# Opening each head's turn with its own block transposes in a streaming attention-backward kernel

## Chip, cores and metric

One core of one Trainium2 chip. The metric is the device time of one execution in microseconds (us). Every number below is of runs in the state called fast; no profiled run fell into another state.

## The reference

Attention with one query per head, and its gradients: 32 heads, 8,192 keys, head size 128, bf16.

```python
def _fwd_reference(q, k, v):                       # q: 1,32,1,128   k, v: 1,32,8192,128
    scale = q.shape[-1] ** -0.5
    scores = jnp.einsum('bhqd,bhkd->bhqk', q, k) * scale
    attn = _softmax(scores, axis=-1)
    return jnp.einsum('bhqk,bhkd->bhqd', attn, v)

def reference(q, k, v, grad_out):                  # cut
    _out, _vjp = jax.vjp(_fwd_reference, q, k, v)
    return (_out, *_vjp(grad_out))                 # out, dq, dk, dv
```

K and V are read once, dK and dV written once: four tensors of 67 MB (64 MiB), 8.39 MB for each head. There is little arithmetic on them.

## The kernel before

One head takes one turn of the loop. Its work is: block transposes of K on the vector engine (`k_blocks`), scores on PE, softmax, V transposed on PE (`v_transposes`), products of V with the output gradient (`v_scores`), then dv as an outer product. dk and dq of a head need a sum over all its products, so they run in the next head's turn. All transfers are issued from one queue: K into three buffers, V into two, each gradient stored in two pieces of 1 MB.

```python
K_BUFS, V_BUFS, NST = 3, 2, 2

for h in range(H + 1):                 # before; softmax details cut
    p_ = h - 1
    k_scores(h); v_transposes(h, 1)
    ds_of(p_); outer(p_, "dk", 0)
    s_mask(h); s_swap(h)
    outer(p_, "dk", 1)                 # stores the first half of dk
    k_blocks(h + 1, 0)                 # next head's K, one stage ahead
    v_transposes(h, 2)
    # ... maximum and its broadcast ...
    v_scores(h, 1)
    outer(p_, "dk", 2); outer(p_, "dk", 3)
    dq_of(p_)                          # last use of K of the head before
    load_k(h + 2)
    # ... exponentials ...
    k_blocks(h + 1, 1); k_blocks(h + 1, 2)
    # ... sum, probabilities, v_transposes(h, 3), v_scores(h, 2) ...
    contract(Vt.pop(h), x["p"], x["m"][:, 2:3])
    for r in range(4):
        outer(h, "dv", r)
    v_scores(h, 3)
    load_v(h + 2)
    v_transposes(h + 1, 0); k_blocks(h + 1, 3); v_scores(h + 1, 0)
```

## Time and profile before

| | before |
|---|---|
| time, median of 3 runs | 675.39 us (674.85 to 675.66) |
| span of the profiled run | 672.6 us |
| one turn, heads 8 to 30 | 20.5 us |

A turn is measured here from the start of one head's masking instruction (the one that writes `sm`) to the next head's.

```profile
180.00:340.00 160.00, 129.75 (x2642) 119.45 (x2640) 123.25 (x156) 41.26 (x79) 0.00 (x0) 0.50 1.01 409
345.00:625.00 280.00, 222.44 (x4584) 205.15 (x4582) 215.41 (x274) 72.75 (x138) 0.00 (x0) 0.54 1.01 411
```

A transfer's completion is recorded once per DMA engine, 16 times in all. Below, **lag** is how much later the last engine finishes a load than the first. The completion records are in the trace, but in none of the page's tables.

### The profile page before, as it was taken

How to read it: one execution, taken by the hardware profiler on the slowest of the kernel's cores; microseconds unless marked ns; L12 is line 12 of the kernel's file. 1: busy time of each engine (PE TensorE's matmuls, PEld its weight loads, DVE VectorE, ACT ScalarE, POOL GpSimd, SP SyncE). 2: the span in 40 equal slices, each digit the busy share in tenths (PEclk: the TensorE clock that was granted, in tenths of full speed). 3: DMA queues.
4: the chain of work that ended last, by engine and by line, in shares of the span. 5: the costliest groups of instructions: out<-in, count | busy, mean ns of one | idle time of the engine just before them, and what ended most of it. 6: DMA issues, size and time to landing. Idle time of an engine off the chain costs nothing.

```text
span 672.6 us, 23041 instructions
## 1 busy us (share of the span) xinstructions
PE 524.4 (78%) x10727; PEld 483.7 (72%) x10727; DVE 508.7 (76%) x658; ACT 172.4 (26%) x321; POOL 0.7 (0%) x6
## 2 busy tenths in 40 slices
PE   3788897878888787878787887878787888877783
PEld 3687786767777777777777777767777777777682
DVE  4678896777787877877777778768777678687766
ACT  1323322222222223222222222222222222222320
POOL 0000000000000000000000000000000000000000
PEclk9975656565555555555555555656556565566665
DMA  8899999999999999999999999999999999999976
GB/s 338 370 382 422 419 427 418 422 427 424 405 410 414 409 411 393 421 416 402 406 412 405 413 413 409 402 416 409 423 419 399 423 399 415 413 396 417 391 292 252
DMA packets 29808, 269.96 MB, mean 401 GB/s; under 512 B 3472, under 2 KB 3472, under 8 KB 6032
## 3 DMA queue, kind: packets, MB, share of 16 engines
q1 hardware_dynamic: 29712, 268.48, 97.6%
q8 instruction: 84, 1.38, 0.8%
q14 instruction: 12, 0.10, 0.0%
HBM read 134.23 MB, written 134.23 MB: 399 GB/s over the span
## 4 chain that ended last, share of the span: by engine, by line
DMA 64%; PE 23%; DVE 8%; ACT 3%; issue 1%; SPq 1%; ACTq 0%; DVEq 0%
DMA Kt<-in_k_dram 64%; PE dp_ps L185 8%; PE T_ps L168 5%; DVE XK_sb L133 5%; PE m_ps L256 3%; PE dp_ps L180 3%; ACT XT_sb L170 2%; PE m_ps L185 1%; PE s_ps L145 1%; DVE diag L254 1%; DVE G_dv L195 1%; DVE G_dk L195 1%; PE m_ps L276 0%; DVE mx L252 0%; ACT p_rep L282 0%
## 5 line engine op out<-in xcount | busy, mean ns | idle before, releaser
L168 PE MATMUL T_ps<-ident,Vt 128*128 128x128 bf16 x2048 | 238.3, 310 | 1.1 <-DMA Vt<-in_v_dram 1.1
L168 PEld LDWEIGHTS <-Vt 128*128 128x128 bf16 x2048 | 218.5, 150 | 7.0 <-issue 5.4
L170 ACT COPY XT_sb<-T_ps 128x1024 f32<-128x1024 f32 x128 | 129.5, 1012 | 334.2 <-PE T_ps L168 334.2
L195 DVE TENSOR_TENSOR G_dv<-p_rep,qd 128x2048 bf16<-128x2048 bf16 x128 | 148.2, 1221 | 77.5 <-ACT p_rep L282 63.4
L133 DVE STREAM_TRANSPOSE XK_sb<-Kt 128x1024 f32<-128x1024 f32 x128 | 155.1, 1230 | 57.2 <-DMA Kt<-in_k_dram 57.2
L195 DVE TENSOR_TENSOR G_dk<-ds_rep,qd 128x2048 bf16<-128x2048 bf16 x128 | 153.2, 1219 | 1.1
L180 PEld LDWEIGHTS <-XT_sb 128*128 128x128 bf16 x2048 | 72.5, 106 | 45.1 <-ACT XT_sb L170 43.8
L180 PE MATMUL dp_ps<-doT,XT_sb 128*128 128x1 bf16 x2048 | 75.1, 166 | 35.3 <-ACT XT_sb L170 35.3
L185 PE MATMUL m_ps<-p_rep,Vt 128*128 128x1 bf16 x2048 | 59.0, 165 | 37.0 <-ACT p_rep L282 37.0
L185 PEld LDWEIGHTS <-Vt 128*128 128x128 bf16 x2048 | 59.5, 104 | 39.0 <-issue 39.0
L145 PE MATMUL s_ps<-q_blk,XK_sb 128*128 128x4 bf16 x2048 | 59.1, 168 | 0.0
L185 PE MATMUL dp_ps<-ds_rep,Kt 128*128 128x1 bf16 x2048 | 58.2, 164 | 0.7 <-issue 0.5
L145 PEld LDWEIGHTS <-XK_sb 128*128 128x128 bf16 x2048 | 57.1, 104 | 0.0
L185 PEld LDWEIGHTS <-Kt 128*128 128x128 bf16 x2048 | 56.2, 101 | 0.8 <-issue 0.6
L256 PE MATMUL m_ps<-diag,ones_f 128*128 128x128 f32 x64 | 21.5, 431 | 38.1 <-DVE diag L254 38.1
L256 PEld LDWEIGHTS m_ps<-diag,ones_f 128*128 128x128 f32 x64 | 13.9, 270 | 45.1 <-DVE diag L254 45.1
L276 PEld LDWEIGHTS m_ps<-rs,ones_f 128*128 128x128 f32 x64 | 15.9, 309 | 25.2 <-ACT qd L211 25.2
L276 PE MATMUL m_ps<-rs,ones_f 128*128 128x1 f32 x64 | 18.6, 360 | 16.4 <-ACT qd L211 16.4
L224 ACT COPY dq_all<-dp_ps 128x1 f32<-128x1 f32 x32 | 5.1, 159 | 93.4 <-PE dp_ps L185 93.4
L151 DVE TENSOR_TENSOR sm<-s_ps,in_quad 128x256 f32<-128x256 f32 x32 | 13.6, 425 | 12.3 <-PE s_ps L145 12.3
L287 ACT COPY o_all<-m_ps 128x1 f32<-128x1 f32 x32 | 5.1, 159 | 61.8 <-PE m_ps L185 61.8
L291 PE MATMUL m_ps<-o_all,do_f 128*128 128x1 f32 x64 | 18.1, 352 | 0.0
(40 smaller groups left out, 160.2 us busy)
## 6 DMA issues: line engine op xcount, KB each, us to landing
Kt<-in_k_dram SPq DMA_DIRECT2D x31, 2048.0 KB, 15.9
out_dram<-G_dv SPq DMA_DIRECT2D x62, 1024.0 KB, 11.8
out_dram<-G_dk SPq DMA_DIRECT2D x62, 1024.0 KB, 11.9
Vt<-in_v_dram SPq DMA_DIRECT2D x30, 2048.0 KB, 16.4
Vt<-in_v_dram SPq DMA_DIRECT2D x8, 512.0 KB, 11.2
Kt<-in_k_dram SPq DMA_DIRECT2D x4, 512.0 KB, 5.2
out_dram<-G_dv SPq DMA_DIRECT2D x4, 512.0 KB, 3.4
out_dram<-G_dk SPq DMA_DIRECT2D x4, 512.0 KB, 4.6
```

Source lines behind the costliest of these rows:

```text
L133: nc.vector.transpose(XK[h][:, :, :, u, :], slots(Kt[h], u, NCH).rearrange("p g d -> p (g d)").bitcast(F32).rearrange("p (g w j) -> p g w ...
L145: nc.tensor.matmul(out[:, g, :], lhsT=cols[:, g, c // 2, c % 2], rhs=q_blk[:, h, c, :], start=(c == 0), stop=(c == 2 * NB - 1), skip_group ...
L151: nc.vector.tensor_tensor(x["sm"][:], x["s"][:, 0:NT].rearrange("p (a g) -> p a g", a=NQ).unsqueeze(2) .to_broadcast([P, NQ, NCH, CH]), in ...
L168: nc.tensor.transpose(T_ps[:, i, :], Vt[h][:, c * CH + i, :], ident[:])
L170: nc.scalar.copy(X.rearrange("p c s -> p (c s)").bitcast(F32), T_ps.rearrange("p c s -> p (c s)").bitcast(F32))
L180: nc.tensor.matmul(st[h]["dp"][:, n:n + 1], lhsT=X[:, i, :], rhs=doT[:, h:h + 1], start=True, stop=True, skip_group_check=True)
L185: nc.tensor.matmul(out_col, lhsT=Xt[:, n, :], rhs=rep[:, n, 0:1], start=(n == 0), stop=(n == NT - 1), skip_group_check=True)
L195: nc.vector.tensor_tensor(slots(G, r, 4).rearrange("p n (a b) -> p n a b", b=R), slots(rep, r, 4).unsqueeze(2).to_broadcast([P, Q, D // R, ...
L254: nc.vector.tensor_scalar(diag[:], ident_f[:], mx[:], scale, op0=ALU.mult, op1=ALU.mult)
L256: nc.tensor.matmul(x["m"][:, 128:256], lhsT=ones_f[:], rhs=diag[:], start=True, stop=True, skip_group_check=True)
L276: nc.tensor.matmul(x["m"][:, 0:1], lhsT=ones_f[:], rhs=rs[:], start=True, stop=True, skip_group_check=True)
L291: nc.tensor.matmul(x["m"][:, 1:2], lhsT=do_f[:, h:h + 1].to_broadcast([P, P]), rhs=o_all[:, h:h + 1], start=True, stop=True, skip_group_ch ...
```

## The change

The intent: one pipeline stage less. A head's block transposes open its own turn, so K is needed later and the first head starts sooner; dq follows its `ds` at once, in two halves; K and V are requested as their buffers fall free, V ahead of the second half of the dv store. The core of it (cut):

```diff
+    def dq_of(h, half):
+        out = st[h]["dp"][:, 128:129]
+        contract(Kt[h], st[h]["ds"], out, half * NT // 2, (half + 1) * NT // 2)
 ...
-            k_scores(h)
+            x = st[h] = {}
+            for u in range(NCH):
+                k_blocks(h, u)
+            v_transposes(h, 0)
             v_transposes(h, 1)
+            k_scores(h)
+            v_scores(h, 0)
 ...                                   (ds, dk 0, mask, swap)
+            dq_of(p_, 0)
             outer(p_, "dk", 1)
-            if more:
-                st[h + 1] = {}
-                k_blocks(h + 1, 0)
-            v_transposes(h, 2)
 ...                                   (maximum)
+            dq_of(p_, 1)
+        if 0 < h and h + 2 < H:
+            load_k(h + 2)
             outer(p_, "dk", 2)
 ...                                   (exponentials, sum)
             outer(p_, "dk", 3)
-            dq_of(p_)
-        if h + 2 < H:
-            load_k(h + 2)
-            k_blocks(h + 1, 1)
-            k_blocks(h + 1, 2)
 ...                                   (V: transposes 2, contraction, products, transposes 3)
-        for r in range(4):
-            outer(h, "dv", r)
         v_scores(h, 3)
+        outer(h, "dv", 0)
+        outer(h, "dv", 1)
         if h + 2 < H:
             load_v(h + 2)
-        if more:
-            v_transposes(h + 1, 0)
-            k_blocks(h + 1, 3)
-            v_scores(h + 1, 0)
+        outer(h, "dv", 2)
+        outer(h, "dv", 3)
```

More of the change, by code (lines that the diff above doesn't have):

```diff
@@ L181, in v_scores, with contract @@
                              start=True, stop=True, skip_group_check=True)
-    def contract(Xt, rep, out_col):
-        for n in range(NT):
+    def contract(Xt, rep, out_col, first=0, last=NT):
+        for n in range(first, last):
             nc.tensor.matmul(out_col, lhsT=Xt[:, n, :], rhs=rep[:, n, 0:1],
@@ L220, in ds_of @@
             in1=x["p_s"][:].unsqueeze(2).to_broadcast([P, NT, R]), op0=ALU.subtract, op1=ALU.mult)
-    def dq_of(h):
-        contract(Kt.pop(h), st[h]["ds"], st[h]["dp"][:, 128:129])
-        nc.scalar.copy(dq_all[:, h:h + 1], st[h]["dp"][:, 128:129])
-    st[0] = {}
-    for u in range(NCH):
-        k_blocks(0, u)
-    v_transposes(0, 0)
-    v_scores(0, 0)
+    def dq_of(h, half):
+        out = st[h]["dp"][:, 128:129]
+        contract(Kt[h], st[h]["ds"], out, half * NT // 2, (half + 1) * NT // 2)
+        if half == 1:
+            nc.scalar.copy(dq_all[:, h:h + 1], out)
     for h in range(H + 1):
         p_ = h - 1
-        x = st.get(h)
-        more = h + 1 < H
         if h < H:
+            x = st[h] = {}
+            for u in range(NCH):
+                k_blocks(h, u)
+            v_transposes(h, 0)
+            v_transposes(h, 1)
             k_scores(h)
-            v_transposes(h, 1)
+            v_scores(h, 0)
         if h > 0:
@@ L257 @@
                              skip_group_check=True)
-            v_scores(h, 1)
+        if h > 0:
+            dq_of(p_, 1)
+        if 0 < h and h + 2 < H:
+            load_k(h + 2)
         if h > 0:
             outer(p_, "dk", 2)
+        if h == 0:
+            load_k(2)
+        if h < H:
+            nbias = small.tile([P, 1], F32, tag="nbias")
+            nc.vector.tensor_reduce(nbias[:], x["m"][:, 128:256], axis=AX.X, op=ALU.max, negate=True)
+            e = small.tile([P, NT], F32, tag="e")
+            rs = small.tile([P, 1], F32, tag="rs")
+            nc.scalar.activation(e[:], x["sn"], ACT.Exp, bias=nbias[:], scale=scale, accum_out=rs[:])
+            rows_bc(h)
+            v_scores(h, 1)
+            nc.tensor.matmul(x["m"][:, 0:1], lhsT=ones_f[:], rhs=rs[:], start=True, stop=True,
+                             skip_group_check=True)
+        if h > 0:
             outer(p_, "dk", 3)
-            dq_of(p_)
-        if h + 2 < H:
-            load_k(h + 2)
         if h == H:
             break
-        nbias = small.tile([P, 1], F32, tag="nbias")
-        nc.vector.tensor_reduce(nbias[:], x["m"][:, 128:256], axis=AX.X, op=ALU.max, negate=True)
-        e = small.tile([P, NT], F32, tag="e")
-        rs = small.tile([P, 1], F32, tag="rs")
-        nc.scalar.activation(e[:], x["sn"], ACT.Exp, bias=nbias[:], scale=scale, accum_out=rs[:])
-        if more:
-            k_blocks(h + 1, 1)
-            k_blocks(h + 1, 2)
-        rows_bc(h)
-        nc.tensor.matmul(x["m"][:, 0:1], lhsT=ones_f[:], rhs=rs[:], start=True, stop=True,
-                         skip_group_check=True)
-        v_transposes(h, 3)
         rinv = small.tile([P, 1], F32, tag="rinv")
@@ L284 @@
         nc.vector.tensor_scalar(x["p_s"][:], e[:], rinv[:], scale, op0=ALU.mult, op1=ALU.mult)
+        v_transposes(h, 2)
+        contract(Vt[h], x["p"], x["m"][:, 2:3])
+        nc.scalar.copy(o_all[:, h:h + 1], x["m"][:, 2:3])
         v_scores(h, 2)
-        contract(Vt.pop(h), x["p"], x["m"][:, 2:3])
-        nc.scalar.copy(o_all[:, h:h + 1], x["m"][:, 2:3])
-        for r in range(4):
-            outer(h, "dv", r)
-        v_scores(h, 3)
+        v_transposes(h, 3)
         nc.tensor.matmul(x["m"][:, 1:2], lhsT=do_f[:, h:h + 1].to_broadcast([P, P]), rhs=o_all[:, h:h + 1],
                          start=True, stop=True, skip_group_check=True)
+        v_scores(h, 3)
+        outer(h, "dv", 0)
+        outer(h, "dv", 1)
         if h + 2 < H:
             load_v(h + 2)
-        if more:
-            v_transposes(h + 1, 0)
-            k_blocks(h + 1, 3)
-            v_scores(h + 1, 0)
+        outer(h, "dv", 2)
+        outer(h, "dv", 3)
     order.__exit__(None, None, None)
```

## The prediction

> **What bounds the kernel now.** I read the page's header, DMA rows and queue table first, then the chain of waits in one period, then busy time by stretches, and last the completion records of single transfers.
>
> ```profile
> span 672.6 us, 23041 instructions
> PE 524.4 (78%) x10727; PEld 483.7 (72%) x10727; DVE 508.7 (76%) x658; ACT 172.4 (26%) x321; POOL 0.7 (0%) x6
> ...
> DMA  8899999999999999999999999999999999999976
> ...
> q1 hardware_dynamic: 29712, 268.48, 97.6%
> q8 instruction: 84, 1.38, 0.8%
> ...
> HBM read 134.23 MB, written 134.23 MB: 399 GB/s over the span
> ```
>
> No compute engine is full; the transfer engines are, except in the first two and last two slices. The chain, merged in order of time, for one head's turn:
>
> ```profile
> 284.22 15.82 DMA Kt<-in_k_dram
> 300.04 0.02 issue
> 300.07 1.25 DVE XK_sb L133
> ...
> 301.80 0.80 PE m_ps L256 x2
> 302.60 0.40 PE dp_ps L180 x16
> 303.00 1.71 PE dp_ps L185 x64
> 304.70 0.03 PE m_ps L207
> 304.74 15.76 DMA Kt<-in_k_dram
> ```
>
> This is a closed loop of 20.52 us: K of two heads on is requested when dq has released its buffer, lands 15.8 us later, and the vector engine's first block transpose of that K waits for it in front of the maximum, the softmax and the next dq. Read alone, it says "latency bound, take K off the loop". The stretches say otherwise (columns: window, its length, busy time of PE, PEld, DVE, ACT, POOL, clock, DMA share, GB/s):
>
> ```profile
> 25.00:45.00 20.00, 16.60 (x344) 15.62 (x343) 15.87 (x21) 5.34 (x10) 0.00 (x0) 0.93 0.91 342
> 45.00:65.00 20.00, 16.82 (x352) 15.70 (x351) 15.81 (x20) 6.08 (x11) 0.00 (x0) 0.50 1.01 424
> 140.28:181.54 41.26, 33.17 (x671) 30.53 (x670) 31.86 (x41) 10.67 (x20) 0.00 (x0) 0.50 1.01 419
> 263.47:304.74 41.27, 33.19 (x671) 30.53 (x670) 31.59 (x41) 10.68 (x20) 0.00 (x0) 0.50 1.01 412
> 633.00:653.00 20.00, 16.70 (x352) 15.46 (x349) 14.98 (x21) 6.07 (x14) 0.00 (x0) 0.58 0.80 321
> 653.00:672.00 19.00, 7.59 (x182) 7.08 (x182) 10.65 (x16) 1.74 (x4) 0.00 (x0) 0.51 0.65 254
> ```
>
> From 45 to 633 us the DMA share is 1.00 to 1.01. A turn needs 8.39 MB (four tensors of 134.2 MB over 32 heads); at 408 to 412 GB/s that is 20.4 to 20.6 us, the turn itself. So the loop and the bandwidth say the same number: the 15.8 us landing is a queueing time, not a latency that earlier requests would remove.
>
> The completion records go one step further. The K load issued at 304.74 finished on its first engine at 313.8, on seven of the 16 by 314.4, on the last at 320.5. Consecutive K loads finished on their first engine at 111.1, 130.8, 150.3, 169.8 (19.5 to 19.7 apart) but on their last at 115.1, 135.9, 156.3, 176.8 (20.5 to 20.8 apart). The fast engines drew ahead until nothing was queued for them; the slowest set the pace from about 98 us on, and it always had a backlog: at 304.74 the last engine still had parts of four earlier transfers to do, until 315.6. One engine's share of a turn is 16 packets of 16 KB at 0.611 us and 32 of 8 KB at 0.309 us, 19.7 us; the other 0.8 us I put down to instruction fetches (about three packets of some 0.93 us a turn over all engines), whose spread over engines I cannot see.
>
> **What the Trainium skill says.** "DMA: Bandwidth & Descriptors", section "Where 436 GB/s comes from": 16 ports give 435 GB/s; this trace's 408 to 427 lies just under it, so little is left. Same page, "Why a DMA increments its semaphore by 16 and not by 1": a transfer runs on up to 16 engines that finish independently, and only the full count means landed; the trace agrees (313.8 to 320.5). "Perfetto Trace Analysis", "Identifying the Most-Contended Engine": DMA occupancy misleads, HBM utilization is to be used; here both agree (97.6%, 399 GB/s). "TensorE: Matmul & The Clock Gate", "What's actually happening": the array runs at half clock when cold. That matters little here: 16 transposes take 1.89 us at granted clock 1.00 (10.8 us) and 1.87 us at 0.50 (306.0 us), so I use one duration for both.
>
> **The change, part by part.** No instruction of the loop is added or removed (dq is cut into two halves of 32 products); order and request times move.
>
> (a) K. Its four block transposes (4 x 1.23 = 4.95 us) move from the turn before, among the softmax steps, to the head's own start. K is still requested after dq of the head before, but needed only at the start of its own turn. The ring of three K buffers then spans three turns = landing + (transposes' start to the end of dq, about 31 us worked from the walk below): at 20.5 us a turn it tolerates a landing of about 30 us instead of 15.8. The 57.2 us that the vector engine waits for K should go.
>
> (b) V. Still two buffers, requested after its last transposes; two turns = landing + about 17.6 us, so up to 23 us are tolerated (median now 16.3). V becomes the ring that binds.
>
> (c) The compute turn. Starting at the score products: 1.7, first dp group 0.6, swap 0.4, half of dq 0.9; the maximum's broadcast waits for the second dk block and the diagonal, to 4.05, then 0.8; half of dq 0.9, rows 0.4, dp 0.6, the sum 0.6: 7.4 us. Transposes 1.85, V contraction 1.75, dp 0.6, transposes 1.9: 13.4. Last dp waits for the scalar engine's copy (1.0): 15.1. Two transpose groups of the next head 3.8: about 18.9 us, with an error of perhaps 0.7. The vector engine's own work is 508.7/32 = 15.9 us, and it should start the next transposes at 12.9 and end at 17.8, before PE needs them. The kernel before ran its early PE-bound turns at 18.3 to 19.4 us (dq to dq), so nothing is won in compute; but it stays under 20.5, so the DMA engines remain the bound and (a) and (b) are hidden in the middle.
>
> (d) Head. Before, the first maximum stands behind the transposes of K of head 1, which waits until 19.58; the first dv store goes at 29.57, V of head 2 at 32.36, while the first loads are done at about 30. Hence the 25 to 45 us hole: (424 - 342)/424 x 20 = 3.9 us of transfer lost. Changed: score products at about 14.7, probabilities 7.5 us later, dv from 22, first store at about 24.4, V request at about 27. The hole closes: -3.9 us.
>
> (e) Tail. Before, V of head 30 landed at 618.9 and the span ended 53.7 us later. Changed: landing, two transpose groups 4.05, two compute turns' distance 19 (head 30 to 31), then from the score products of head 31 to its last dk 20.6 (before: 644.1 to 666.6 = 22.5), then the 6.0 us of last store and output: 49.7 us. That is 4 us less; V also goes ahead of the second half of the dv store, which is worth up to 1.2 us of queue. Against it: the last 4.2 MB (10.2 us at 410) cannot start before head 31's dv, and 15.7 MB precede them, so transfers alone end near 662. I count -4.5 us.
>
> Sum: 675.4 - 3.9 - 4.5 = 667.0 us.
>
> **Rivals.** First, a real gain in the middle: packets are slow (0.7 to 1.2 us for 16 KB) mostly in the part of a turn when little is queued; with deeper queues these vanish and the turn falls to about 20.0 us: 26 turns x 0.5 = 13 us more, 654. For it: 419 to 424 GB/s early, when queues were deeper. Against: the last engine's spacing was 20.5 us even then, so the higher rate was the fast engines' lead. Second, PE becomes the bound: if my 18.9 us is really 21, 32 x 0.5 = 16 us more, about 683. For it: 16.4 us of PE work and a strictly ordered queue with several hand-offs. Against: every step is a measured duration and the sum has 1.6 us to spare. Third, the store and request order on the one issuing queue: the second dv half now stands behind the V request, which waits for PE until about 13.4 us, when that half is ready at 12.9; cost below 1 us and hidden. Fourth, head and tail gains are masked by the slowest engine's fixed work: 672 to 675.
>
> **Range and chances.** The middle term (about 590 us) is unchanged within 1%, so +-6 us; head and tail give 3 to 10 us. Range 659 to 675. A gain over 2% (under 661.9) needs part of the first rival: 0.16. A loss over 2% (over 688.9) needs the second in full: 0.03. Within 2%: 0.81.
>
> **What would show it.** Right: DMA share 1.00 in the middle with turns of 20.4 to 20.6 us, no vector wait for K of size, K landings longer than 15.8 us or idle in their buffer, waits moved to V; the first dv store near 24 us; no hole at 25 to 45 us; about 50 us from V of head 30 to the end. Wrong: a DMA share well below 1 in the middle (compute turn too long), or turns of 20.0 us and below with share 1 (the slowest engine does profit from deeper queues).

## More of the kernel before

The prediction shows the busy times and the chain. Three more places matter later. First, from the list of waits (engine, line and what it waited for: us in total, times, longest): the vector engine waits for K, PE almost never for V.

```profile
DVE XK_sb L133 <- DMA Kt<-in_k_dram: 57.2, 29, 3.0
...
PEld L168 <- DMA Vt<-in_v_dram: 1.5, 1, 1.5
```

Second, the table of transfers (last column: median us from request to landing). Third, two stretches of the middle (window, length, busy time of PE, PEld, DVE, ACT, POOL, clock, DMA share, GB/s): both halves run at the same rate.

```profile
Kt<-in_k_dram SPq DMA_DIRECT2D x31, 2048.0 KB, 15.9
...
Vt<-in_v_dram SPq DMA_DIRECT2D x30, 2048.0 KB, 16.4
```

## The result, and the profile after

The changed kernel took **679.74 us** (678.06 to 681.02, 4 runs), the kernel before 675.12 us in the same rounds. The ratio is 1.0066, with a 95% interval of 1.0043 to 1.0090. A ratio is the mean time of one kernel's fast runs over that of the other's of the same rounds, so it is not quite the ratio of the medians quoted. It is within 2%, as predicted most likely, but slower rather than faster, and outside the predicted range.

The page after. Compare the GB/s row, in 40 slices of 17 us, with the rate in the prediction's stretches of before:

```profile
span 679.2 us, 23039 instructions
...
DMA  8999999999999999999999999999999999999874
GB/s 335 421 415 422 427 419 424 425 424 419 414 425 425 429 424 425 426 425 421 417 413 392 391 390 415 388 378 379 404 385 394 393 383 413 391 397 376 353 319 182
```

There is no hole at the start: 415 to 427 GB/s from the second slice on. Up to the twentieth slice (340 us) the rate is higher than before's, mostly 419 to 429. Then it falls to about 390. The same stretches as above show it:

```profile
180.00:340.00 160.00, 128.97 (x2658) 122.69 (x2659) 122.03 (x157) 42.56 (x79) 0.00 (x0) 0.59 1.01 423
345.00:625.00 280.00, 212.76 (x4355) 202.00 (x4355) 203.59 (x260) 70.85 (x130) 0.00 (x0) 0.54 1.00 393
```

The DMA share is 1.01 and 1.00. So the engines are "busy" all the time while they move 7% less: the packet records are longer. A reader who trusts the share alone sees nothing.

The wait has moved from K to V, and landings have become longer (waits, then transfers):

```profile
PEld L168 <- DMA Vt<-in_v_dram: 92.7, 27, 4.7
...
DVE XK_sb L133 <- DMA Kt<-in_k_dram: 2.5, 1, 2.5
```

```profile
Kt<-in_k_dram SPq DMA_DIRECT2D x31, 2048.0 KB, 21.9
...
Vt<-in_v_dram SPq DMA_DIRECT2D x30, 2048.0 KB, 25.4
```

In the chain (start, us, what), V's landing takes the place that K's had. One loop of V covers two turns:

```profile
258.60 25.09 DMA Vt<-in_v_dram
...
299.74 25.05 DMA Vt<-in_v_dram
...
340.74 27.16 DMA Vt<-in_v_dram
...
383.97 26.98 DMA Vt<-in_v_dram
...
427.01 27.79 DMA Vt<-in_v_dram
```

From one V to the next it is 41.1 us at 258.60 to 299.74, two turns of 20.6. After 340.74 it is 43.0 to 43.2, two turns of 21.6. The extra 2 us a loop are in the landing: 25.1 became 27.0 to 27.8.

Where the time went, from the start times of the masking instruction:

```
                     before     after    after - before
head 0                16.1       16.1        0.0
head 16              337.7      330.0       -7.7
head 30              625.5      633.4       +7.9
head 31              646.0      650.8       +4.8
end of the span      672.6      679.2       +6.6
turns 8 to 16         20.5       20.5
turns 16 to 30        20.6       21.7
```

The profiled run of after is the slowest of its four (681.0 us). So the head gained 7.7 us, all by head 6; turns 17 to 30 lost 15.6; the end won back 1.3. Net +6.6.

The completion records show what goes with the loss. The lag of before grows from 2 us to 7 by 170 us and stays there. After, it grows by about 1.0 us a turn, from 3.7 us at 119 us to 13.9 at 325 and 16 at 346, and stays there. From then on the last engine finishes some 9 us after the last but one; the other 15 lie within about 6 us of each other (before: 1 and 6). Moving its part of a V load takes the slowest engine 4.87 us between 180 and 330 us, and 5.98 us after 345 (before: 4.95 and 4.94); its part of K stays at 4.88. This one term is the 1.1 us by which the turn grew.

Long load packets are not the slowest engine's alone. Of all 16 KB load packets, 1.3% took over 0.7 us between 180 and 330 us and 21% between 345 and 605 us, while 8 KB store packets stayed at 0.31 us. The kernel before has 13% and 11% all along, and its slowest engine is spared. Part of this must be waiting that the records count as busy: once the lag stands still, the quick engines go at the slowest one's pace, 20.5 or 21.7 us a turn instead of the 19.5 that they took while it grew, and yet the share reads 1.00.

### The profile page after: what moved, and what is told of

It reads as the page before. It is cut to its first block, busy times and chain, and to the rows that moved or that the text cites. A ratio compares the mean times of both kernels' runs of the same rounds, so it can differ in the third digit from the quotient of the medians.

```text
span 679.2 us, 23039 instructions
## 1 busy us (share of the span) xinstructions
PE 524.0 (77%) x10727; PEld 497.6 (73%) x10727; DVE 508.7 (75%) x658; ACT 175.8 (26%) x321; POOL 0.7 (0%) x6
## 3 DMA queue, kind: packets, MB, share of 16 engines
q8 instruction: 83, 1.36, 0.7%
## 4 chain that ended last, share of the span: by engine, by line
DMA 51%; PE 39%; DVE 7%; ACT 1%; issue 1%; SPq 0%
DMA Vt<-in_v_dram 50%; PE T_ps L168 20%; PE m_ps L185 5%; PE s_ps L145 5%; DVE G_dk L195 4%; PE dp_ps L180 3%; PE dp_ps L185 2%; PE m_ps L253 2%; PE m_ps L271 2%; DVE sm L151 1%; PE m_ps L207 1%; ACT XT_sb L170 1%; DVE diag L251 1%; DMA Kt<-in_k_dram 1%; DVE mx L249 0%
## 5 line engine op out<-in xcount | busy, mean ns | idle before, releaser
L168 PE MATMUL T_ps<-ident,Vt 128*128 128x128 bf16 x2048 | 233.6, 311 | 90.4 <-DMA Vt<-in_v_dram 88.8
L168 PEld LDWEIGHTS <-Vt 128*128 128x128 bf16 x2048 | 216.2, 149 | 93.0 <-DMA Vt<-in_v_dram 92.7
L195 DVE TENSOR_TENSOR G_dk<-ds_rep,qd 128x2048 bf16<-128x2048 bf16 x128 | 155.8, 1219 | 1.1
L133 DVE STREAM_TRANSPOSE XK_sb<-Kt 128x1024 f32<-128x1024 f32 x128 | 148.1, 1213 | 2.6 <-DMA Kt<-in_k_dram 2.5
L180 PEld LDWEIGHTS <-XT_sb 128*128 128x128 bf16 x2048 | 64.1, 103 | 36.7 <-ACT XT_sb L170 27.6
L185 PEld LDWEIGHTS <-Kt 128*128 128x128 bf16 x2048 | 63.6, 102 | 6.9 <-issue 2.9
L185 PE MATMUL dp_ps<-ds_rep,Kt 128*128 128x1 bf16 x2048 | 64.5, 165 | 1.4 <-issue 0.9
L185 PEld LDWEIGHTS <-Vt 128*128 128x128 bf16 x2048 | 61.1, 105 | 0.0
L253 PE MATMUL m_ps<-diag,ones_f 128*128 128x128 f32 x64 | 24.7, 488 | 11.0 <-DVE diag L251 11.0
L253 PEld LDWEIGHTS m_ps<-diag,ones_f 128*128 128x128 f32 x64 | 15.4, 300 | 13.9 <-DVE diag L251 13.9
L280 ACT ACTIVATE p_rep<-e,rinv 128x256 bf16<-128x256 f32 x32 | 16.3, 508 | 29.2 <-DVE rinv L278 29.2
L278 DVE RECIPROCAL rinv<-m_ps 128x1 f32<-128x1 f32 x32 | 5.4, 168 | 23.6 <-PE m_ps L271 23.6
L218 DVE SCALAR_TENSOR_TENSOR ds_rep<-dp_ps,pdt,p_s 128x256 bf16<-128x256 f32 x32 | 15.5, 484 | 4.4 <-PE dp_ps L180 1.1
## 6 DMA issues: line engine op xcount, KB each, us to landing
Kt<-in_k_dram SPq DMA_DIRECT2D x31, 2048.0 KB, 21.9
Vt<-in_v_dram SPq DMA_DIRECT2D x8, 512.0 KB, 13.9
```

The lines of the kernel that those rows point to most:

```text
L133: nc.vector.transpose(XK[h][:, :, :, u, :], slots(Kt[h], u, NCH).rearrange("p g d -> p (g d)").bitcast(F32).rearrange("p (g w j) -> p g w ...
L168: nc.tensor.transpose(T_ps[:, i, :], Vt[h][:, c * CH + i, :], ident[:])
L180: nc.tensor.matmul(st[h]["dp"][:, n:n + 1], lhsT=X[:, i, :], rhs=doT[:, h:h + 1], start=True, stop=True, skip_group_check=True)
L185: nc.tensor.matmul(out_col, lhsT=Xt[:, n, :], rhs=rep[:, n, 0:1], start=(n == 0), stop=(n == NT - 1), skip_group_check=True)
L195: nc.vector.tensor_tensor(slots(G, r, 4).rearrange("p n (a b) -> p n a b", b=R), slots(rep, r, 4).unsqueeze(2).to_broadcast([P, Q, D // R, ...
L218: nc.vector.scalar_tensor_tensor(out=x["ds"][:], in0=x["dp"][:, 0:NT].unsqueeze(2).to_broadcast([P, NT, R]), scalar=pdt[:], in1=x["p_s"][: ...
```

## The experiments

Two questions. Why do the engines drift apart, and why does the turn lengthen when they have? The expectations name theories by letters. Every run had 3 rounds; "before" in the same rounds was 674.5 to 675.0 us.

### Which buffer catches the engines that run ahead

**A third V buffer**, V requested one head earlier.

```diff
-V_BUFS = 2
+V_BUFS = 3
 ...
             load_k(2)
+            load_v(2)
 ...
-        if h + 2 < H:
-            load_v(h + 2)
+        if h + 3 < H:
+            load_v(h + 3)
```

> The changed kernel with a third V buffer and V requested one head earlier. Theory A (V ring of two buffers exhausted by the slow engine's lag): 44 us of landing are then tolerated, the turn stays at 20.5 us to the end, about 665 us (662 to 669). Theory C (the limit is the eight completion semaphores, that is, a transfer may not be issued before the eighth before it has landed, 27 us at six a turn): still a slow regime from about head 17, 674 to 682 us, with the issuing queue waiting for landings rather than PE waiting for V. Rival D (the second half is slow for a reason of its own: heat, addresses): also 676 to 682 us, with the slow turns beginning at the same head.

Measured: 661.50 us (661.36 to 662.05), ratio to before 0.9811 (0.9794 to 0.9827). No long turns: 20.3 us from 8 to 16 and 20.4 from 16 to 30, although the lag grows to 20 us. The wait on V is gone and K is the one that is waited for:

```profile
DVE XK_sb L133 <- DMA Kt<-in_k_dram: 75.4, 26, 3.5
...
PEld L168 <- DMA Vt<-in_v_dram: 1.5, 1, 1.5
```

A wait of 75 us, more than before's 57, in a kernel that is 1.9% faster: the wait is only where the slowest engine's pace becomes visible. It follows that the ring of V buffers is part of the loss, and that a deep lag alone does not stretch packets.

**The block transposes put back** into the turn before, everything else of the change kept.

```diff
+            if more:
+                st[h + 1] = {}
+                k_blocks(h + 1, 0)        # 1, 2 and 3 likewise at their old places
-            for u in range(NCH):
-                k_blocks(h, u)
```

> The changed kernel with one part undone: the vector engine's block transposes of the next head go back among the softmax steps of the turn before, so K has to land within about 16 us. Theory A: the K ring caps the slow engine's lag at about 7 us as in the kernel before, no turn of 21.6 us appears, turns are 20.5 us throughout; total 668 to 675 us. If the slow regime has nothing to do with how far the lag may grow (rival D), turns of 21.6 us from head 17 on remain and the total is 678 us or more.

Measured: 662.20 us (660.76 to 662.57), ratio 0.9814 (0.9799 to 0.9829), better than I expected. K catches the leaders at a lag of 9 to 10 us, PE does not wait for V (1.5 us in all), and turns average 20.1 us up to head 16 and 20.3 after it. A store of 1 MB takes the slowest engine 2.60 us here, against 2.69 in the changed kernel. So the part of the change that gave it its name is the one that costs, and undoing it alone wins 2.5% over the changed kernel (0.9814 / 1.0066). The rest of the change is a gain.

**The kernel before with a fourth K buffer**, K one head earlier: its K ring loosened by another way.

> The kernel before with a fourth K buffer and K requested one head earlier. If the kernel before, too, loses time because its K ring catches the lag (at 7 us) and not because of the slowest engine's own pace: turns fall from 20.5 to 20.2 us once loads no longer bind, 662 to 668 us. If its 20.5 us were the slowest engine's own pace, as my prediction said: no change in the middle, 671 to 676 us. V with two buffers may become the catcher; then slow turns appear late.

Measured: 677.43 us (675.02 to 681.28), ratio 1.0044 (1.0003 to 1.0086). The middle keeps 20.5 us a turn up to head 16, so the K wait of before hid no time. Then V becomes what PE waits for (61.1 us), the lag reaches 11 to 12.6, the slowest engine's V takes 5.49 us and turns average 21.2. The long turns are not special to the changed kernel's order: loosening K is enough.

**The kernel before with a third V buffer** (the same edit as above).

> The kernel before with a third V buffer, V requested one head earlier: the one thing that made the changed kernel 2.7 % faster. Theory A (in the kernel before the K ring catches the leading engines at a lag of 7 us, and the turn is the slowest engine's own 20.5 us; V never held anything): 673 to 677 us, turns 20.5 us, the wait on K still about 57 us. Rival (the third V buffer is a gain of its own, whatever the order): 658 to 666 us.

Measured: 675.67 us (675.34 to 676.22), ratio 1.0017 (1.0000 to 1.0033); turns 20.5 us, lag about 7. As theory A said, V never held anything before, so a V buffer buys nothing there; the vector engine's wait on K stays (61.8 us).

### When and in which order the loads are requested

**Stores of 2 MB** instead of 1 MB, in the changed kernel and in the one before.

```diff
-NST = 2
+NST = 1
```

> The changed kernel with stores of 2 MB (16 KB rows) instead of 1 MB (8 KB rows); nothing else. Theory A: one of the 16 transfer engines is slower on stores by a cost per packet (1 MB takes it 2.70 us against 2.47 on the others, 28 ns for each of 8 packets), it sets the turn of 20.5 us, and its growing lag uses up the V buffers at head 17, after which turns take 21.6 us. Half the packets: its turn falls to about 20.1 us, the lag grows half as fast, the slow regime comes late or never: about 656 us (650 to 664). Theory B: the slow engine is slower per byte: turns 20.5 then 21.6 as now, 676 to 684 us. Theory C: the deep lag comes from the number of outstanding transfers (eight completion semaphores in rotation, six transfers a turn): with four a turn no slow regime, but turns of 20.5: about 664 to 668 us.

Measured: 669.12 us (668.00 to 671.48), ratio 0.9926 (0.9903 to 0.9948). It hits none of the three numbers. On the slowest engine a store takes as long per byte as in 1 MB pieces (5.3 to 5.4 us for 2 MB against 2.7 for 1), so its slowness is no cost per packet. Turns are 20.5 up to head 23 and 20.8 to 21.5 after; V still catches, at a lag of 14 to 16. The long turns only begin later.

> The kernel before with stores of 2 MB instead of 1 MB. Theory A with the cost per packet: the slowest engine needs 4 x 0.22/2 = 0.45 us less a turn: 20.05 us, about 661 us (656 to 666). Theory B (slower per byte): no change, 673 to 678 us. If the loop of K (landing plus compute) is the bound rather than the slowest engine's pace, 2 MB stores come later and the loop lengthens: 676 us or more.

Measured: 679.02 us (678.75 to 679.93), ratio 1.0070 (1.0055 to 1.0085). Here coarser stores cost: at head 16 the kernel is 4.6 us behind before's, and the distance does not grow after it (turns 20.5). It is also the one run in which the last engine's V takes long (5.55 us on average: mostly 4.9, every third 6.4) with turns of 20.5. But the last two engines finish within 0.5 us of each other here, so this figure may mix two engines, and I draw nothing from it.

**V requested about 5 us later** (after a one-element read of the old V in the next turn).

```diff
+            late = small.tile([P, 1], BF16, tag="late")
+            nc.vector.tensor_copy(late[:], Vt[p_][:, NT - 1, D - 1:D])
+            if h + 1 < H:
+                load_v(h + 1)
 ...
-        if h + 2 < H:
-            load_v(h + 2)
```

> The changed kernel with V requested about 5 us later (a one-element read of V by the vector engine behind ds holds the buffer). The two V buffers then tolerate a landing of about 20 us instead of 25, so the slowest engine's lag is caught at 8 to 11 us instead of 14 to 17. Theory G (what matters is how far the lag gets before a ring catches it: deep lag makes the slowest engine's V load run while the other 15 load K, and its V takes 6.0 us instead of 4.9): turns of 20.2 to 20.6 us to the end, 662 to 668 us. Theory F (V as the ring that catches is bad in itself, because V gates PE and with it everything): the ring is tighter, turns of 21.6 us or more start earlier, near head 9: 682 us or more.

Measured: 679.73 us (678.42 to 681.25), ratio 1.0074 (1.0047 to 1.0101). The lag stops growing at 11 to 12 us at about 235 us, yet turns stay at 20.5 up to head 16 and are 21.0 to 22.1 from 17 on; the slowest engine's V takes 4.89 us in the first part and 5.80 in the second. Both theories missed: neither the depth of the lag, nor the moment at which the ring catches, starts the long turns.

**K requested directly ahead of V**, about 9 us later than in the changed kernel.

```diff
-        if 0 < h and h + 2 < H:
-            load_k(h + 2)
 ...
         if h + 2 < H:
+            if h > 0:
+                load_k(h + 2)
             load_v(h + 2)
```

> The changed kernel with K requested directly before V instead of after dq, some 9 us later, so that the three K buffers tolerate about 20 to 22 us of landing and K, not V, catches the lag, at about 11 us. Theory G and theory F both allow turns of 20.2 to 20.6 us here: 662 to 670 us. If turns of 21.6 us appear with K as the catcher too, both are wrong about the catcher and the two loads standing together in the queue are what costs: 680 us or more.

Measured: 669.75 us (669.15 to 670.11), ratio 0.9924 (0.9902 to 0.9947). PE still waits for V, 81.9 us against 92.7, and the lag is 13 to 14, but turns are 20.6 except for two single ones (22.0 and 21.9), and the slowest engine's V takes about 5.0 us.

With the same buffers and the same catcher, only K's place in the queue, and with it the time of its request, is different. This suggested overlap as the cause: in the changed kernel, while the slowest engine moves V, 58% of the other engines' time goes to K (28% in this run).

**K requested directly behind V.**

> The changed kernel with the request of K moved behind that of V (the earlier run had it directly ahead of V and gave 669.8 us). Theory of overlap (turns grow to 21.6 us because the slowest engine, half a turn behind, moves its V while the other 15 move the next K): with K next to V the others are at stores half a turn later, so the slowest engine's V takes under 5.1 us, turns stay at 20.5 to 20.7 us, 667 to 673 us. Rival (what helped was only that K had landed before V was caught up, or a later K request keeps the lag smaller): V is caught as in the changed kernel, turns of 21 us and more from head 17 on, 677 to 682 us. If K itself comes too late, a wait of the vector engine on K of over 30 us shows it.

Measured: 665.14 us (664.98 to 665.36), ratio 0.9859 (0.9845 to 0.9874), turns 20.5 and V on the slowest engine 4.92, as the overlap theory said. But it is a weak test. K now comes so late that it is the catcher, as the last sentence of the expectation allowed for:

```profile
DVE XK_sb L133 <- DMA Kt<-in_k_dram: 92.5, 29, 4.2
```

And it holds evidence against the theory. Between 120 and 340 us the others spent 52% of the slowest engine's V time on K, nearly what they do in the changed kernel, and that V took 4.88 us. Overlap alone does not stretch anything.

### Is it the place in the memory?

In five kernels with different histories the first long turn, or a single long one, was that of head 17 or 18, about the middle of the tensors. So I moved the heads by sixteen. (The single long one has a plainer cause where I could follow the packets, in the kernel before, in the changed one and in before with a third V buffer: a packet of instructions from a second queue, q14, stands among the slowest engine's V packets of that turn, at 342.9 us in the changed kernel and 349.6 in before. It does not say why the turns stay long.)

```diff
+    def at(h):
+        return (h + 16) % H
 ...                                 (and so for q, grad_out and the output columns)
-        return x[0, h].rearrange(...)
+        return x[0, at(h)].rearrange(...)
```

> The changed kernel with the heads taken in the order 16 to 31, then 0 to 15; everything else, results too, as before. Theory P (place: loads or stores in the upper half of the tensors are stretched when the lag is deep): the second half runs at 20.5 us a turn, because it now works on the lower half of the tensors, and the time is 664 to 670 us, unless the first half turns slow (then up to 675). Theory D (depth or time: what counts is that the engines are 15 us apart, from 340 us on): turns of 21.3 to 22 us from the seventeenth turn on as before, 678 to 682 us.

Measured: 673.18, 681.08, 681.32 and 673.78 us, median 677.43, ratio 1.0041 (0.9979 to 1.0103), no difference clear of the noise; two levels from one kernel on one chip. The profiled run is one of the quicker ones: turns of about 20.5 us up to the sixteenth, 20.5 to 21.2 from 17 to 23, and 21.1 to 21.8 from 24 to 30, the V of the slowest engine 5.41 us. The second half, now on the lower half of the tensors, is again the slow one.

Loads of heads 16 to 31 taken from heads 0 to 15 (`h % 16`; a wrong result):

> Wrong on purpose: the changed kernel with K and V of heads 16 to 31 loaded from heads 0 to 15 once more; stores unmoved. If the place of the loads in the memory matters: no long turns, 662 to 670 us. If the place of the stores, or time or depth alone: long turns from head 17 on as before, 677 to 682 us.

Measured: 677.25 us (675.87 to 679.07), ratio 1.0041 (1.0018 to 1.0064); turns 16 to 30 21.35 us, V on the slowest engine 5.61.

Only the stores moved by sixteen heads (a wrong result):

> Wrong on purpose: the changed kernel with loads in order and each head's gradients stored sixteen heads away (heads 16 to 31 first). If the place of the stores matters: the second half runs at 20.5 us, 664 to 670 us. If the place of the loads, or time or depth alone: as the changed kernel, 677 to 682 us. If what counts is the distance between loads and stores, something else than either.

Measured: 677.60 us (674.99 to 678.18), ratio 1.0037 (1.0013 to 1.0061); 21.39 us and 5.73.

The V-delayed kernel with the heads rotated:

> The V-delayed kernel (679.7 us, its lag at 11 to 12 us from 235 us on, long turns only from head 17 on) with the heads rotated by sixteen. Theory P: long turns as soon as the lag is deep, that is in the turns 11 to 16, and 20.5 us from the seventeenth on; about 5 us lost instead of 15, 667 to 673 us. Theory D: turns 20.5 us up to the sixteenth and 21.3 and more after it, 678 to 682 us.

Measured: 680.78 us (678.53 to 682.42), ratio 1.0088 (1.0057 to 1.0119). Turns 11 to 16 are 20.5 to 20.7 with the lag already at 11 to 12, turns 17 to 30 average 21.6. Between 280 and 345 us the others are on K for 58 to 65% of the slowest engine's V, and it takes 4.88 to 4.89 us; from 365 us on, with no more overlap than that, 5.5 and above. Place in the memory is refuted by all four, and overlap once more.

### Why the engines drift apart

**Transfers alone**: the same loads and stores in the same order, no arithmetic (a wrong result).

```python
for h in range(H + 1):              # zero: a constant tile
    if h > 0:      store(h - 1, out_2, 0)
    if h + 2 < H:  load_k(h + 2)
    if h > 0:      store(h - 1, out_2, 1)
    if h == H:     break
    store(h, out_3, 0)
    if h + 2 < H:  load_v(h + 2)
    store(h, out_3, 1)
```

> Wrong result on purpose: the loads and stores of the changed kernel in its order and sizes, with the same buffers, stores from one tile of zeros and no computation (next to no instruction fetches). Theory H (one engine is slower because it fetches the instructions): no engine lags, every engine does a turn in 19.7 us, about 634 us (630 to 640). Theory I (one engine, or stores beside loads, is slower by itself): a lag that grows by 0.5 us a turn as with computation, 648 to 660 us. In both cases the time is the floor of any order of this work on one queue.

Measured: 636.89 us (636.66 to 637.23), ratio 0.9438 (0.9413 to 0.9462). Every engine takes 2.46 us for a 1 MB store and 4.85 for a load, 19.54 us a turn, and the lag stays at 3.3 us. No engine is slower by itself. But this run takes away the arithmetic and the instruction fetches together, so two more runs separate them.

**The same with 10,700 small products** on constant tiles, tied to nothing: the kernel's number of PE instructions, and no vector work.

```diff
+    for n in range(10700):
+        nc.tensor.matmul(acc[:, 0:64], lhsT=sq[:], rhs=zero_flat[:, 0:64], ...)
```

> Wrong on purpose: the loads and stores alone, as in the run of transfers without arithmetic (636.9 us), with 10,700 small matrix products beside them that nothing waits for; they touch the on-chip memory little (one constant square), but bring about as many PE instructions as the kernel has. Theory H (instruction fetches, which share the transfer engines, make one engine fall behind by some 0.5 us a turn): the slowest engine falls behind all through, by 10 to 20 us in 32 turns, and the time is 645 to 660 us. Rival J (the falling behind comes from the arithmetic's own use of the on-chip memory): lag as without arithmetic (about 3 us, constant) and 635 to 640 us.

**The same with 2,200 wide products and 650 vector copies**: about the kernel's busy time on PE and the vector engine, in a quarter of the instructions.

```diff
+    for n in range(2200):
+        nc.tensor.matmul(acc[:, 0:512], lhsT=sq[:], rhs=zero_flat[:, 0:512], ...)
+    for n in range(650):
+        nc.vector.tensor_copy(X[:], src[:])         # 2,048 elements a partition
```

> Wrong on purpose: the same loads and stores with about as much busy time of PE and of the vector engine as the kernel has, but in few instructions: 2,200 wide products and 650 vector copies of 2,048 elements a partition. Theory H: about a quarter of the fetches, so the lag grows by 0.1 to 0.15 us a turn and the time is 638 to 643 us. Rival J: the vector engine's reads and writes beside the transfers make the lag grow as in the kernel, 645 to 660 us.

Measured: 659.74 us (659.08 to 663.00), ratio 0.9789 (0.9764 to 0.9814), with many instructions, and 640.60 us (640.41 to 640.93), ratio 0.9496 (0.9482 to 0.9510), with few. The lag grows to 20 us by 440 us in the first, and to 6.4 by 517 us in the second. (The expectations' 0.5 us a turn is the growth in the kernel from one load to the next; a turn has two loads, so it is 1.0.) From the pages (queue, kind: packets, MB, share), the transfers alone, many instructions, few instructions:

```profile
span 635.3 us, 254 instructions
...
q1 hardware_dynamic: 29136, 268.48, 99.8%
```

```profile
span 657.6 us, 21656 instructions
...
q1 hardware_dynamic: 29136, 268.48, 97.8%
q8 instruction: 83, 1.36, 0.7%
```

```profile
span 638.6 us, 5307 instructions
...
q1 hardware_dynamic: 29136, 268.48, 99.4%
q8 instruction: 17, 0.28, 0.2%
```

This settles that the drift comes with the number of instructions and not with how long the engines are busy. The run with the vector engine busy for 396 us and PE for 478, but 5,307 instructions and 17 fetch packets on q8, is 3.7 us above the transfers alone. The run with PE busy for 368 us and nothing else to speak of, but 21,656 instructions and 83 packets, is 22.9 us above them. Rival J is refuted.

That the fetch packets themselves hold the slowest engine back, as theory H has it, is not shown, and the packet records speak against its plain form. They name no engine, but on one engine a packet starts within about 3 ns of the end of the one before, so most can be followed. A fetch packet takes its engine some 0.95 us, and the packet behind it takes about 0.69 us instead of 0.31 (8 KB) or 1.16 instead of 0.61 (16 KB). At 1.3 to 1.5 us for the two together, the slowest engine would have to carry some 16 of the 83 for the 22.9 us (an estimate from these numbers). Of those that can be followed to the end of their transfer, between 100 and 600 us, 4 of 63 are on the engine that completes it last; in the kernel before it is 1 of 50, in the changed kernel 5 of 46. The slowest engine is slow in another way: most of its store packets are a little long. In the kernel before it takes 2.68 us for a store of 1 MB, against 2.46 in the transfers alone, in packets of 0.31 to 0.40 us instead of 0.309; a K load takes 4.89 against 4.85. Four stores, K and V (4.95) make 20.56 us, its whole turn. So something that comes with the instructions stretches these packets. Whether it is the fetches in a roundabout way or anything else that every instruction brings, no run separates.

The Trainium skill describes the fetching. "Runtime: NRT & Kernel Launch", section "Instruction fetch mechanics", says that instructions are refilled in blocks of 16 KiB through a DMA queue of the sequencer's own, and that this is mostly hidden. The block size agrees (1.36 MB in 83 packets is 16.4 KB each). "Hidden" is not the whole story where the DMA engines are the bound: each packet takes one of them for some 0.95 us, and the stream of instructions, fetches included, costs 3.6% of 636.89 us.

The run of many products also gives a floor, as an estimate: these transfers in this order with about as many instructions take about 660 us. The two best kernels here, at 661.50 and 662.20 us, are within 3 us of it.

### The runs together

"Catcher" is the load that an engine waits for; lag, V and turns are of the second half of the run (345 to 605 us; heads 16 to 30).

| kernel | us | catcher | lag | V on the slowest engine | turn |
|---|---|---|---|---|---|
| before | 675.1 | K | 7 | 4.94 | 20.6 |
| before, third V buffer | 675.7 | K | 7 | 4.95 | 20.6 |
| before, stores of 2 MB | 679.0 | K | 5 | 5.55 (see there) | 20.5 |
| before, fourth K buffer | 677.4 | V | 12 | 5.49 | 21.2 |
| changed | 679.7 | V | 16 | 5.98 | 21.7 |
| changed, V later | 679.7 | V | 13 | 5.80 | 21.6 |
| changed, stores of 2 MB | 669.1 | V | 15 | 5.15 | 20.8 |
| changed, K directly ahead of V | 669.8 | V | 13 | 5.05 | 20.8 |
| changed, K directly behind V | 665.1 | K | 11 | 4.92 | 20.5 |
| changed, transposes put back | 662.2 | K | 10 | 4.95 | 20.3 |
| changed, third V buffer | 661.5 | K | 14 to 21 | 4.86 | 20.4 |

The six with K as catcher have no stretch of long turns. Those with V as catcher have long turns, from two single ones to all of the second half, and how long depends on where K stands in the queue and on the size of the stores.

## Why the prediction was wrong, and where it was right

**What bounds the kernel** was right, and more firmly than it was put: the DMA engines, and among them the slowest. The fourth K buffer left turns at 20.5 us up to head 16, so that is the slowest engine's own pace and not the K loop's latency. That the extra load comes with the instructions was right as well. But the 0.8 us were put down to fetch packets, and what the trace shows on the slowest engine is stretched stores (4 x 0.22 us); how the instructions cause that stays open. ("Four tensors of 134.2 MB" is a slip: they are 67.1 MB each, and the 8.39 MB a turn are right.)

**(a) K** was right: the wait fell from 57.2 to 2.5 us.

**(b) V as the ring that binds** was right as a statement of who waits. The step that failed is the one taken from it, "the middle term (about 590 us) is unchanged within 1%": turns 17 to 30 took 21.7 us instead of 20.5, 15.6 us in all. The prediction took the time of a packet as given and asked only whether V's landing, 16.3 us before, stays under a tolerance of 23 us. That test could not decide it, since the landing of a ring that binds grows until it fills its tolerance: V landed after 25.0 us from 115 us on, and PE waited for it in every turn (23.5 us in all between 180 and 340 us) while turns stayed at 20.5. What went on changing was the lag. K's ring had been what kept the 15 quick engines from running further ahead; once (a) had loosened it, the lag grew by 1.0 us a turn until V's two buffers held them, at about 340 us. The prediction had the parts of this in hand: it had seen the fast engines draw ahead until nothing was queued for them. It did not ask what the change would do to that limit.

Reaching the V ring would still have been free if packets had kept their duration. They did not: the slowest engine's V went from 4.87 to 5.98 us, which is the turn's growth. Taking away the V limit (third buffer), restoring the K limit (transposes back) or moving K's request removed most or all of it. **Why the packets get longer stays open.** Depth of the lag alone, overlap with the others' K alone, and place in the memory were each tested and refuted. What remains is a description: V as the catcher, K requested early in the turn, and not before about 330 us, in whichever order the heads come. One rival was not tested: that load packets stretch when the quick engines run out of queued requests, and that the slowest engine's V then falls among them; the rising share of long load packets (1.3 to 21%) fits it, but the kernel before has 11 to 13% of them without this harm. The rotated kernel's two levels, 673 and 681 us, say that the state is not even entered to the same degree in every execution.

**(c) The compute turn** was mis-sized: 18.9 us predicted, 17.3 to 17.4 measured in turns 2, 3 and 31, which no transfer holds up. "Nothing is won in compute" was wrong.

**(d) The head** was right in mechanism, the hole is gone, but 3.9 us became 7.7. The missing part goes with (c): turns 1 to 6 took 108.0 us in sum instead of 115.9, and the first of them, at 16.4 to 17.4 us, were not bound by transfers yet.

**(e) The tail** gave 1.3 us, not 4.5 (from head 30's masking to the end 47.1 us before, 45.8 after; by the prediction's own mark, from the landing of head 30's V, 53.7 became 51.1, not 49.7). The last turn is short, as predicted, but from head 31's masking to the end it now takes 28.4 us instead of 26.6: I take it that the slowest engine, 15 us behind, still has stores to do; no run separates this.

**The sum** as it should have been: 675.1 - 7.7 + 15.6 - 1.3 = 681.7, against 679.7 measured; the 2.0 us difference is that the profiled runs compared here, 674.4 and 681.0 us, lie 0.8 below and 1.3 above the medians.

**The rivals.** The first, a gain in the middle with deeper queues, is the surprise: it is wrong for the changed kernel, but two single edits to it, a third V buffer or the transposes put back, reach turns of 20.1 to 20.4 and 661.5 to 662.2 us, so the slowest engine does profit somewhat. The second named 683 us, near the measured time, but by a PE-bound turn of 21 us, which (c) refutes: a right number for a wrong reason. The fourth, head and tail gains that are masked, did not happen: the lead of 7.7 us stood up to head 16.

## What to carry to other kernels

Where the transfers are the bound, look at how far apart the 16 engines finish one load, and ask which buffer ring keeps the quick ones from running ahead; loosening that ring does not speed the slowest engine, and hands the limit to the next ring, so give that one a buffer as well. Measure the floor with the transfers alone and once more with the instruction stream beside them, before you value any wait: here a kernel with a wait of 75 us was faster than one with 57, and the floor with the instruction stream was 23 us above that without. And read the rate beside the DMA share, since shares of 1.01 and 1.00 stood over 423 and 393 GB/s.

## What the Trainium skill lacked or had wrong

- "Runtime: NRT & Kernel Launch", section "Instruction fetch mechanics": fetching is called mostly hidden. Where transfers are the bound, each fetch packet took a DMA engine for some 0.95 us, and the stream of instructions that brought 83 of them cost 22.9 us of 659.7 (one that brought 17 cost 3.7). How much of this the fetches cost by themselves is not shown.
- "DMA: Bandwidth & Descriptors", section "Latency and other measured facts": that certain engines are usually slower is put, as a guess, down to descriptor rings of transfers that GpSimd issues. This kernel issues none from GpSimd, and its one slow engine comes with the stream of instructions: lag 3.3 us without it, 20 with it. Which engine it is, the trace does not say.
- No page says how far the engines of one queue can drift apart under load, and that buffer counts limit it: 7 us before, 16 after, up to 21 with a third V buffer.
- "Perfetto Trace Analysis", section "Identifying the Most-Contended Engine": it rightly warns of DMA occupancy, but not that it stays full when packet records get longer: share 1.01 at 423 GB/s, 1.00 at 393.
- No page explains load packets that lengthen (4.87 to 5.98 us for the slowest engine's part of 2 MB) with queues and sizes unchanged, and no run here does either.
